# Gate products of the first 128 tokens taken ahead of the norms of the next two tiles, in an attention and gated-MLP kernel

## The chip, the cores and the metric

The kernel runs on one core of a Trainium2 chip. The metric is the device time of one execution in microseconds; the median over runs is quoted. A core has five engines, named as in the profile: PE (TensorE, matmuls; PEld is its loading of weights), DVE (VectorE), ACT (ScalarE), POOL (GpSimd) and SP (SyncE, which here issues DMA transfers). Each engine works through its own queue in order; a wait for another engine or a transfer holds everything behind it.

## The reference

Four batches of eight heads, 768 tokens, head size 64. Attention sees a window of 16 neighbours and 24 block summaries; its output goes through a norm and a gated MLP with weights 512 x 1536, 512 x 1536 and 1536 x 512.

```python
k_sum = k.reshape(B, H, nb, 32, D).max(axis=3)
v_sum = v.reshape(B, H, nb, 32, D).mean(axis=3)
scores_l = where(|i - j| < 16, q @ k.T / sqrt(D), -1e9)
scores_s = q @ k_sum.T / sqrt(D) + log(32)
a = softmax(concat(scores_l, scores_s))
x = a @ concat(v, v_sum)                          # 3072 tokens x 512
xn = x / sqrt(mean(x * x) + 1e-6) * rms_g
g = xn @ w_gate
out = (g * sigmoid(g) * (xn @ w_val)) @ w_out     # all in float32
```

## The kernel before

**Tiles and groups.** The 3072 tokens are 24 tiles of 128, six to a batch. A tile's attention gives `x` (128 tokens x 512); the norm turns it into `xT`, the transposed tile as an f16 pair of a high and a low half. The MLP works on groups of tiles, `GROUPS` = 384, 128, 256 and six times 384 tokens: group 0 is tiles 0 to 2, group 1 tile 3, group 2 tiles 4 and 5. A product of two f32 matrices is three f16 matmuls, high x high, high x low and low x high, summed in one PSUM bank.

**The first batch.** Attention of tiles 0 to 5 is done by the `su_` steps in f32. Meanwhile the gate and value weights arrive in chunks, are decoded by `decode` (ACT L542, DVE L543 and L544; ACT L570 then takes their sum of squares) and split into f16 halves by `split_gv` (L573: small matmuls L576 and L579, then ACT L589 and DVE L590). The output weights are decoded later, with the same `decode` lines and the sums of squares of `row_o` (ACT L632, DVE L629).

**The norm.** `norm_a` (L1105) takes the sum of squares of `x` (ACT L1110, DVE L1112, POOL L1113). `norm_b` (L1116) scales it (DVE L1121). For tiles 0 to 2 PE transposes it (four matmuls, L1129) into a bank `acc`, ACT casts the bank to the high half of `xT` (`copy`, recorded at L431) and DVE subtracts to get the low half (`sub`, L436).

**The gate.** `gate_val grp f T` (L1271) computes chunk f, 128 of the 1536 columns, for the T tokens of one group: 12 matmuls (L1284) for the gate and 12 for the value, each 128 columns of weights by T tokens. ACT L1291 takes the tanh, DVE L1292 and L1294 form `h`; groups 0, 1 and half of group 2 keep `h` until the output weights are ready (`halve` L1300, `project` L1306, matmuls L1316). Banks are `gv` (2) or, for odd chunks of the first two groups, `acc` (3). From group 5 on `seven` (L1206) does the products with seven block products in place of eight.

**Later batches.** Attention reads transposed f16 operands that SP fetches by transposing DMAs: `qT` (L801), `kT` (L734), `eT` (L863) and `xT` (L1137). Scores are PE L839, the product with the values PE L880. Sums over blocks of k and v are folded from tiles `hn` (`sum_load` L662, its DMA L671; `sum_fold` L674: ACT L681 and, for the v sums, POOL L687 and L692); PE L704 adds the sums of squares.

**What sets the order.** `PLAN` (L43) is a string of steps in the order in which they are recorded. `WARM` (L41) gives some steps a number of filler matmuls (L746, 128x256 of ones) that keep TensorE busy. After recording, `in_order` (L334) puts each engine's instructions into the order that `ORDER` (L148) lists for it: one table of numbers each for PE, ACT, DVE, POOL and SP. So the recorded order decides which buffers an instruction gets, and the tables decide what it is queued behind.

## Time and profile before

| | us |
|---|---|
| median of 3 runs | 706.69 |
| the runs | 705.15, 706.69, 710.21 |
| the profiled execution's own time | 705.49 |
| its span | 703.7 |

The profiled execution is 1.8 us longer than its span (what lies before the first and after the last instruction) and 1.20 us below the median. The mean granted clock of TensorE is 0.995 of full speed. PE is the busiest engine, 673.9 us or 96% of the span; DVE follows with 549.5, ACT with 494.2, POOL with 220.7. To read the profile: a row of the timeline gives start, length, engine, line, operation, output<-input, partitions x elements and, in brackets, how long the engine stood still before it and what ended that wait. Matmuls overlap: of a run of n equal ones the spacing is the run's length less one matmul's, divided by n - 1.

### The profile page before, as it was taken

Reading aid. Unit: us, or ns where it says so; the run is one execution under the profiler, and the core shown is the slowest. Engines: PE = TensorE matmul, PEld = TensorE weight load, DVE = VectorE, ACT = ScalarE, POOL = GpSimd, SP = SyncE. Lnnn points to the kernel's source line nnn. Section 1 sums busy time; section 2 is a strip of 40 time slices with the busy share of each in tenths; the row PEclk is TensorE's granted clock in tenths of the full one; section 3 lists DMA queues with packets and bytes.
Section 4 is the critical chain, followed back from the end, with each engine's and each line's share of the span. In section 5 each row is a group of like instructions: output and inputs, shape, how many; then the busy total and the mean of one; then the engine's idle time right before and its main releaser. Section 6 shows DMA issues by size and latency. Waiting matters only on the chain.

```text
span 703.7 us, 16081 instructions
## 1 busy us (share of the span) xinstructions
PE 673.9 (96%) x5854; PEld 480.9 (68%) x5854; DVE 549.5 (78%) x1611; ACT 494.2 (70%) x1083; POOL 220.7 (31%) x321
## 2 busy tenths in 40 slices
PE   7898999979989899999999999999999999999997
PEld 5585767866546665555655655877888698779874
DVE  3798889799888776757989988999887878675443
ACT  3597866668887778647677786858889767834432
POOL 4465222550334353513133533432133213410000
PEclk9999999999999999999999999999999999999999
DMA  9999562736588978767458966282949553330001
GB/s 202 287 332 283 187 211 72 130 67 113 105 162 189 164 157 162 139 143 154 104 114 161 172 149 129 64 157 59 161 80 172 130 94 62 78 51 16 32 16 46
DMA packets 243860, 93.32 MB, mean 133 GB/s; under 512 B 227717, under 2 KB 227717, under 8 KB 243781
## 3 DMA queue, kind: packets, MB, share of 16 engines
q1 hardware_dynamic: 239172, 84.78, 58.3%
q10 hardware_dynamic: 3456, 6.29, 2.5%
q0 software_dynamic: 1152, 1.22, 0.7%
q8 instruction: 46, 0.75, 0.5%
q14 instruction: 34, 0.27, 0.1%
HBM read 50.45 MB, written 6.59 MB: 81 GB/s over the span
## 4 chain that ended last, share of the span: by engine, by line
PE 65%; DVE 11%; DMA 8%; ACT 7%; issue 3%; POOL 2%; SPq 2%; ACTq 0%; DVEq 0%; POOLq 0%
PE acc L1316 18%; PE gv L1216 16%; PE gv L1284 15%; PE acc L1284 3%; DMA eT<-ee 2%; PE att L880 2%; PE att L839 2%; DMA qT<-qs 2%; PE att L1052 1%; DMA hn<-in_k_dram 1%; PE gv L746 1%; POOL ee L436 1%; DVE sm L843 1%; SPq L750 1%; DMA v2f<-in_v_dram 1%
## 5 line engine op out<-in xcount | busy, mean ns | idle before, releaser
L1316 PE MATMUL acc<-wo,hhl 128*128 128x512 f16 x864 | 228.6, 379 | 0.0
L1284 PE MATMUL gv<-xT,w_gv 128*128 128x384 f16 (+2 forms) x1296 | 215.6, 304 | 4.0 <-DVE h L1294 2.0
L1284 PEld LDWEIGHTS <-w_gv 128*128 128x128 f16 x1584 | 141.3, 99 | 77.1 <-issue 8.9
L1316 PEld LDWEIGHTS <-hhl 128*128 128x128 f16 x864 | 81.5, 98 | 61.9 <-issue 1.1
L436 POOL TENSOR_TENSOR ee<-sm,ee 128x256 f16<-128x256 f32 (+1 forms) x72 | 70.7, 995 | 164.6 <-ACT ee L431 142.5
L1216 PEld LDWEIGHTS <-w_gv 128*128 128x128 f16 x1008 | 87.3, 98 | 13.1 <-DMA xT<-xs 1.0
L854 ACT ACTIVATE sm<-sm,mx,c 128x192 f32<-128x192 f32 x144 | 70.7, 538 | 1.6
L1216 PE MATMUL gv<-S,w_gv 128*128 128x192 f16 x504 | 63.6, 246 | 0.0
L843 DVE CUSTOM_DVE_ANT_0 sm<-att,mask 128x192 f32<-128x192 f32 x144 | 44.7, 351 | 15.8 <-PE att L839 9.1
L1216 PE MATMUL gv<-xT,w_gv 128*128 128x192 f16 x504 | 55.2, 246 | 0.6 <-DMA xT<-xs 0.6
L1216 PEld LDWEIGHTS <-wo 128*128 128x128 f16 x540 | 46.9, 98 | 5.5 <-issue 0.4
L1216 PE MATMUL gv<-xT,wo 128*128 128x192 f16 x360 | 49.0, 246 | 0.0
L880 PE MATMUL att<-vv,eT 128*128 128x65 f16 x720 | 43.0, 193 | 4.8 <-DMA eT<-ee 2.4
L880 PEld LDWEIGHTS <-eT 128*128 128x128 f16 x720 | 34.6, 97 | 14.7 <-DMA eT<-ee 3.9
L839 PE MATMUL att<-kT,qT 128*128 128x192 f16 x288 | 41.2, 246 | 3.5 <-DMA qT<-qs 3.0
L1284 PE MATMUL acc<-xT,w_gv 128*128 128x384 f16 (+1 forms) x288 | 42.6, 272 | 1.9 <-DVE h L1292 1.0
L436 POOL TENSOR_TENSOR xs<-x,xs 128x512 f16<-128x512 f32 x21 | 24.5, 1167 | 49.5 <-ACT xs L431 49.4
L681 ACT ACTIVATE junk<-hn 96x512 uint8<-96x512 f32 x48 | 30.0, 624 | 10.8 <-DMA hn<-in_v_dram 6.0
L431 ACT CAST ee<-sm 128x512 f16<-128x512 f32 (+1 forms) x72 | 34.8, 507 | 1.8 <-DMA eT<-ee 1.0
L839 PEld LDWEIGHTS <-qT 128*128 128x128 f16 x288 | 25.7, 98 | 15.1 <-DMA qT<-qs 4.3
L1113 POOL TENSOR_TENSOR x_r<-x_r,consts 128x1 f32<-128x1 f32 x24 | 19.8, 826 | 49.3 <-DVE x_r L1112 41.7
L687 POOL TENSOR_TENSOR hn<-hn 96x512 f32<-96x512 f32 x18 | 24.7, 1370 | 27.5 <-DMA hn<-in_v_dram 16.5
...
## 6 DMA issues: line engine op xcount, KB each, us to landing
...
```

The costliest lines, as they stand in the source:

```text
L431: nc.scalar.copy(o, i)
L436: (nc.vector if ENG.get(op, "p") == "v" else nc.gpsimd).tensor_tensor(o, a, b, op=ALU.subtract)
L681: nc.scalar.activation(junk[0:96], y[:, o:o + DM], AF.Square, accum_out=d["ss"][:, j:j + 1])
L687: eng.tensor_tensor(x[:, 0:w], x[:, 0:w], y[:, 0:w], op=op)
L839: nc.tensor.matmul(pt[:, j * SC:(j + 1) * SC], lhsT=s["qT"][:, a * H + h, :], rhs=kT[:, h, :], start=(a == 0), stop=(a == 1))
L843: nc.vector.tensor_tensor_reduce(sm[:, i, :], pt[:, j * SC:(j + 1) * SC], mask, 1.0, NEG, op0=ALU.add, op1=ALU.max, accum_out=mx[:, i:i + 1])
L854: nc.scalar.activation(sm[:, i, :], sm[:, i, :], AF.Exp, scale=s["c"][:, 0:1], bias=mx[:, i:i + 1])
L880: nc.tensor.matmul(po[r][:, h // 2, 0:D + 1], lhsT=e, rhs=vv[:, 0:D + 1], start=(n == 0), stop=(n == len(pairs) - 1))
L1113: nc.gpsimd.tensor_tensor(r, r, nhalf, op=ALU.pow)
L1216: nc.tensor.matmul(bank[:, i * T2:(i + 1) * T2], lhsT=right(n, wi, c), rhs=left(xi, c), start=start, stop=(i == 1 and c == 1 and wi == 1), ...
L1284: nc.tensor.matmul(pt[:, 0:T], lhsT=w_gv[:, f - f % 2 + i, wi, c, f % 2, :], rhs=x[:, xi, c, 0:T], start=(n == 0), stop=(n == 3 * NC - 1))
L1316: nc.tensor.matmul(accs[grp][j], lhsT=h[:, js], rhs=wo_hl[f // 2][:, wi, f % 2, :], start=(f == first and n == 0), stop=(f == (first - 1) ...
```

## The change

- `gate_val` is taken apart into `gate_banks` (takes the PSUM banks and issues the fillers), `gate_part` (the 24 matmuls of columns a to b), `gate_head` (banks, and the part of columns 0 to 128) and `gate_val` (the rest, and all that follows).
- `PLAN` gets two steps: `gate_head 0 0` after tile 2's attention and before the norms of tiles 2 and 1, and `gate_head 0 1` after these norms. Chunks 0 and 1 of group 0 are thus computed for tile 0 first and for tiles 1 and 2 later: 48 matmuls of 128x384 become 48 of 128x128 and 48 of 128x256.
- In all gate products of `gate_part` the loop over the three half products is now outside and that over the four row blocks of the weights inside, and the low half of the tokens comes last.
- `WARM`: the fillers of `norm_b 1` and `norm_b 2` go from 8 to 4 each; the 4 of `gate_val 0 0 384` go to `gate_head 0 0`. In all 116 fillers become 108.
- The five tables of `ORDER` are new throughout. Beside these 48 matmuls and 8 fillers with their weight loads no instruction comes or goes; line numbers grow by 2, behind `gate_val` by 14.

```diff
-WARM = {... "norm_b 0": 4, "norm_b 1": 8, "norm_b 2": 8, "gate_val 0 0 384": 4}
+WARM = {... "norm_b 0": 4, "norm_b 1": 4, "norm_b 2": 4, "gate_head 0 0": 4}
-split_gv 3; su_attend 2 1; norm_a 2; norm_a 1; decode_gv 4; load_gv 10; norm_b 2; norm_b 1; su_v2 3; split_gv 4;
+split_gv 3; su_attend 2 1; gate_head 0 0; norm_a 2; norm_a 1; decode_gv 4; load_gv 10; norm_b 2; norm_b 1; gate_head 0 1; su_v2 3; split_gv 4;
 ORDER = dict(
     PE="""
-0x22 36 -37x20 4x6 -10x4 6x4 3 -4x2 8x4 -10x2 1 1 -4 7 -7 6x3 1 -2 1x3 25 -22x2 -6 5x2 4x2 15 -4 -19x3 4 17 -23 4 35
+58x2 -60x58 2 5x2 -7 1 1 -4 1 14x2 -13x2 11 -12x4 1 -2 2 -2 1 52 -49 7x2 -9x4 16 27 -28 -12 -7 -7 23 -12x2 11 1 -4 1
...
-        def gate_val(grp, f, T):
-            x = xT[grp]
+        heads = {}
+        def gate_banks(grp, f, T):
             def bank():
                 if grp < KEEP and f % 2:
                     return ps.tile([P, 512], F32, name="acc", bufs=3)
                 return ps.tile([P, 512], F32, name="gv", bufs=2)
             pg = bank()
             warm(pg)
-            pg, pv = (pg[:, 0:T], pg[:, T:2 * T]) if T <= 256 else (pg, bank())
-            for i, pt in ((0, pg), (1, pv)):
+            return (pg[:, 0:T], pg[:, T:2 * T]) if T <= 256 else (pg, bank())
+        def gate_part(grp, f, banks, a, b):
+            x = xT[grp]
+            for i, pt in enumerate(banks):
                 n = 0
-                for c in range(NC):
-                    for (wi, xi) in ((0, 0), (0, 1), (1, 0)):
-                        nc.tensor.matmul(pt[:, 0:T], lhsT=w_gv[:, f - f % 2 + i, wi, c, f % 2, :], rhs=x[:, xi, c, 0:T],
-                                         start=(n == 0), stop=(n == 3 * NC - 1))
+                for (wi, xi) in ((0, 0), (1, 0), (0, 1)):
+                    for c in range(NC):
+                        nc.tensor.matmul(pt[:, a:b], lhsT=w_gv[:, f - f % 2 + i, wi, c, f % 2, :], rhs=x[:, xi, c, a:b],
+                                         start=(n == 0), stop=(n == 3 * NC - 1), skip_group_check=True)
                         n += 1
+        def gate_head(grp, f):
+            heads[grp, f] = gate_banks(grp, f, groups[grp])
+            gate_part(grp, f, heads[grp, f], 0, P)
+        def gate_val(grp, f, T):
+            pg, pv = heads[grp, f] if (grp, f) in heads else gate_banks(grp, f, T)
+            gate_part(grp, f, (pg, pv), P if (grp, f) in heads else 0, T)
```

Place 1, PE around the transposes of tile 0 (L1129 before, L1131 after). Before, they are followed by eight fillers (L746; one pair of rows stands for them) and the small matmuls of a weight split:

```order
L1129 MATMUL acc<-ident,x 128x128 x4
L746 LDWEIGHTS ones
L746 MATMUL acc<-ones 128x256
...
L576 MATMUL att<-w_ss,ones 128x1
L579 LDWEIGHTS w_gv
L579 MATMUL att<-consts,w_gv 128x1
```

After, on PE at the same place:

```order
L1131 MATMUL acc<-ident,x 128x128 x4
L748 LDWEIGHTS ones
L748 MATMUL acc<-ones 128x256
...
L748 MATMUL gv<-ones 128x256
L1290 LDWEIGHTS w_gv
L1290 MATMUL gv<-xT,w_gv 128x128
```

Two fillers and then the first gate matmul of tile 0 stand in front of the small matmuls (now L578 and L581); the rest of the 48 follow among the later fillers, splits and transposes, and the first 128x256 one stands behind all of them.

The same place on ACT, before: three decodes (L542), the two squares of `norm_a` (L1110), then the sums of squares of the weights (L570) around the casts of `xT` (L431).

```order
L542 ACTIVATE w_985<-wo_459 128x1024
L1110 ACTIVATE junk,x_ss<-x 128x512 x2
L570 ACTIVATE w_gv,w_ss<-w_813 128x1024
L570 ACTIVATE w_gv,w_ss<-w_877 128x1024
L431 CAST xT<-acc 128x4x128
L570 ACTIVATE w_gv,w_ss<-w_985 128x1024
L431 CAST xT<-acc 128x4x128 x2
```

After, on ACT (all lines 2 higher):

```order
L544 ACTIVATE w_1025<-wo_459 128x1024
L1112 ACTIVATE junk,x_ss<-x 128x512 x2
L433 CAST xT<-acc 128x4x128
L572 ACTIVATE w_gv,w_ss<-w_843 128x1024
L572 ACTIVATE w_gv,w_ss<-w_925 128x1024
L572 ACTIVATE w_gv,w_ss<-w_1025 128x1024
L433 CAST xT<-acc 128x4x128
```

The cast of tile 0 has moved in front of two sums of squares.

Place 2, DVE where group 1's gate ends and group 2's first bank (`gv`) is waited for: the last two decodes (L544), sums of squares (L629, an ISA row each with one that reads the sum) and the products of group 1 (L1292, L1294). Before:

```order
L544 SCALAR_TENSOR_TENSOR wo_1348<-wo_1348,w_2062 128x1024
L544 SCALAR_TENSOR_TENSOR wo_1484<-wo_1484,w_2139 128x1024
L629 ISA th,scales<-wo_1072 128x512
L629 ISA scales 128x1
L1292 SCALAR_TENSOR_TENSOR h_227<-h_227,gv 128x128
L1294 SCALAR_TENSOR_TENSOR h_227<-h_227,gains,gv 128x128
```

After, on DVE (L546, L631, L1306, L1308):

```order
L546 SCALAR_TENSOR_TENSOR wo_1388<-wo_1388,w_2102 128x1024
L1306 SCALAR_TENSOR_TENSOR h_227<-h_227,gv 128x128
L546 SCALAR_TENSOR_TENSOR wo_1524<-wo_1524,w_2179 128x1024
L1306 SCALAR_TENSOR_TENSOR h_227<-h_227,gv 128x128
L631 ISA th,scales<-wo_1216 128x512
L631 ISA scales 128x1
L1308 SCALAR_TENSOR_TENSOR h_227<-h_227,gains,gv 128x128 x2
```

One sum of squares (`wo_1112`) has gone ahead of the decodes, another (`wo_1216`) has come in front of the last product L1308.

Place 3, SP around the fourth of the transposing loads of `qT`. Before:

```order
L1137 DMA_TRANSPOSE xT<-xs 128x8x128
L671 DMA hn<-in_k_dram 96x512
L734 DMA_TRANSPOSE kT<-khl 128x8x128
L863 DMA_TRANSPOSE eT<-ee 128x12x128
L671 DMA hn<-in_k_dram 96x512
L801 DMA_TRANSPOSE qT<-qs 128x16x128
```

After, on SP (L736, L1139, L673, L865, L803):

```order
L736 DMA_TRANSPOSE kT<-khl 128x8x128
L1139 DMA_TRANSPOSE xT<-xs 128x8x128
L673 DMA hn<-in_k_dram 96x512
L865 DMA_TRANSPOSE eT<-ee 128x12x128
L803 DMA_TRANSPOSE qT<-qs 128x16x128
L673 DMA hn<-in_k_dram 96x512
```

The load of `qT` is now issued in front of the second load of `hn`.

## Rows read from the trace of the kernel before

**Rows 1.** The page, part 1: busy us, share of the span, instructions of each engine.

```profile
PE 673.9 (96%) x5854; PEld 480.9 (68%) x5854; DVE 549.5 (78%) x1611; ACT 494.2 (70%) x1083; POOL 220.7 (31%) x321
```

**Rows 2.** The waits of PE, longest sums first.

```profile
PE att L576 <- ACT w_gv L570: 3.4, 3, 2.5
PE att L839 <- DMA qT<-qs: 3.0, 2, 1.7
...
PE att L704 <- ACT junk L681: 1.8, 1, 1.8
```

**Rows 3.** Windows of 2 us: PE, PEld, DVE, ACT, POOL busy, granted clock, DMA share, GB/s.

```profile
54.00:56.00 2.00, 0.00 (x0) 0.00 (x0) 2.00 (x4) 1.97 (x7) 0.15 (x1) 1.00 1.09 336
...
58.00:60.00 2.00, 2.00 (x18) 1.76 (x17) 1.81 (x7) 0.98 (x3) 0.74 (x4) 0.58 1.09 299
60.00:62.00 2.00, 2.00 (x18) 1.99 (x17) 1.12 (x4) 1.06 (x2) 1.86 (x8) 0.57 1.12 289
```

**Rows 4.** The timeline of PE, 48 to 66 us.

```profile
52.04 0.60 PE L1129 MATMUL acc<-ident,x 128*128 128x128 f32 x4
...
56.04 0.38 PE L576 MATMUL att<-w_ss,ones 128*128 128x1 f32 x2 [2.52 <-ACT w_gv L570]
...
58.80 1.06 PE L1129 MATMUL acc<-ident,x 128*128 128x128 f32 x4
...
62.27 0.33 PE L1284 MATMUL gv<-xT,w_gv 128*128 128x384 f16 x1
...
64.11 2.11 PE L1284 MATMUL gv<-xT,w_gv 128*128 128x384 f16 x12
```

**Rows 5.** The timeline of ACT, 48 to 66 us.

```profile
54.85 1.04 ACT L570 ACTIVATE w_gv<-w 128x1024 bf16<-128x1024 f32 x1
...
56.93 0.56 ACT L431 CAST xT<-acc 128x512 f16<-128x512 f32 x1
```

**Rows 6.** The timeline of PE, 141 to 158 us.

```profile
148.33 0.22 PE L1284 MATMUL gv<-xT,w_gv 128*128 128x128 f16 x1
...
148.83 1.11 PE L1284 MATMUL gv<-xT,w_gv 128*128 128x128 f16 x17
151.77 0.39 PE L704 MATMUL att<-kv_ss,ones 96*128 96x8 f32 x2 [1.82 <-ACT junk L681]
...
153.62 4.56 PE L1284 MATMUL gv<-xT,w_gv 128*128 128x256 f16 x25 [1.39 <-DVE h L1294]
```

**Rows 7.** The timeline of PE, 228 to 236 us.

```profile
228.54 1.47 PE L1284 MATMUL gv<-xT,w_gv 128*128 128x256 f16 x12
...
230.28 0.27 PE L1284 MATMUL gv<-xT,w_gv 128*128 128x256 f16 x1
232.28 0.83 PE L839 MATMUL att<-kT,qT 128*128 128x192 f16 x8 [1.73 <-DMA qT<-qs]
```

**Rows 8.** The timeline of DVE, 141 to 158 us.

```profile
146.87 4.43 DVE L544 SCALAR_TENSOR_TENSOR wo<-wo,w 128x1024 uint32<-128x1024 uint32 x2
151.22 1.75 DVE L629 CUSTOM_DVE_ANT_0 th<-wo 128x512 bf16<-128x512 f32 x1
...
153.21 0.35 DVE L1294 SCALAR_TENSOR_TENSOR h<-h,gains,gv 128x128 f32<-128x128 f32 x1
...
153.68 0.95 DVE L629 CUSTOM_DVE_ANT_0 th<-wo 128x512 bf16<-128x512 f32 x1
```

**Rows 9.** The timeline of POOL, 141 to 158 us.

```profile
146.44 1.52 POOL L687 TENSOR_TENSOR hn<-hn 96x512 f32<-96x512 f32 x1 [2.09 <-DMA hn<-in_v_dram]
147.93 1.15 POOL L436 TENSOR_TENSOR xs<-x,xs 128x512 f16<-128x512 f32 x1
```

**Rows 10.** The timeline of DVE, 48 to 66 us.

```profile
53.35 2.35 DVE L544 SCALAR_TENSOR_TENSOR w<-wo,w 128x1024 uint32<-128x1024 uint32 x2
```

**Rows 11.** The timeline of SP's DMA queue, 206 to 226 us.

```profile
224.17 0.76 SPq L671 DMA_DIRECT2D hn<-in_k_dram  x1
225.01 3.96 SPq L801 DMA_TRANSPOSE qT<-qs  x1
```

More of the change, by code (lines that the diff above doesn't have):

```diff
@@ new lines @@
+-11x3 8x4 -12x2 10 -107 -55 2 44 6 105 -111 -3 2 3 -4 117x5 7 -8 7x3 -10 9 -10x5 5 -24 -116 138x4 2 3 -4 -29 28x2 1x3
+-41 6 -7 29x2 -29 54 -52 -7 44 12 3 -4x3 -16 50 89 -121x2 -6 5 -6 -26 58 10x2 -12x3 9x2 -11 10x2 -112 111 -51 37x3 10
+-11x3 -39x2 5x2 -13 -25 29x2 5 -6x2 4x2 -6 10 -6x5 1 3 24 -75 45x3 1x4 -57 147 -148 5 70 -75 74 69 -142 5x2 -5x3 -5
+142x3 -5 -71x3 68 -69x2 70 -71x2 6 -7 20 -21 5 -6x2 4x2 -6 -82 5 75 4x8 4 -5x2 4x2 10x3 -19 27 -10 9 -10 9x2 -29 111x2
+2 -88 -12x4 8x2 -10x3 -18 106x2 1x3 -88x5 -34 4 -5 5 -6x2 2 1 108 -57 11x2 -13x3 10x2 -12x4 8 -9x3 6 -36 2 -3 27 6x4
@@ new lines @@
+191 -54 53 -13x3 10 -11 -188 197 -11 10x2 -12 11 -12 11 -12 11x2 -66 3 -4x2 3 11x2 33 -47 -3 3 -2 45 -40 39 10 -51 -5x2
+-4 11 -12 5 -4 52 -45 -4 5 2 -3 4 -3 2 -6 2 48 -46 -12x2 -5 12 46x4 -49 1 46 -18 17x3 -20 19 -20 19x2 -21x9 24x12
+-24x12 24x12 -24x12 24x10 -22 21 -22 21 -22x10 24x6 -143 142x2 -20x3 17 -18x2 16 -17x3 14 -15x4 11 -147x3 -4 147x4 -155
+162 -9x4 5 -6 5 -6 5 -6x2 4x2 6 -7x6 4 -4 3 -4x2 2x2 58x2 10 -11x2 9 -10 9 -10x3 7x2 -9 8x3 -11 10 -11 -69 68 -69x5 4
+-5 72x3 -42x2 40x4 -44 43 7 -8x2 -78 77 5 -6x4 2 -90x2 34 -32x2 -5 4x3 3x4 -7x3 4x3 3x2 -5x3 5 -4 3x3 -6x2 4 57 -49
@@ new lines @@
+3x3 -6x2 -121x2 119 5 -3x2 1 41x2 10x4 -14 13 -14 -172 14 111x3 42 -157 156 11 -12x2 10 -11x3 8x2 -54x4 -9x4 5 -6 -122
+131x2 -7 6 -7 6 -7 6 -7 35 9 -46 -152 196x2 -198 14x2 6 -7 2 177x2 10 -11x5 6 -7x2 5 -6x3 3 44x2 2x4 -6x2 -48 7 -8x3
+5x4 -9x2 7 -8x2 6x6 -72 -7 2x2 73 11 -12 11x2 -13x3 10x2 -12x3 9x2 -92 -5 95 -12 11 -12x3 9x3 -100 4x2 110 11x2 -13x2
+-113 123 -12x2 10x2 -12x2 10x2 -12x2 75 -76x3 7x3 -126 125 -130 130x2 -3 2x3 -132 131x7 -142 -4 6 -4 -4 143 11 -12x4 8
+-9x4 5 -6x3 37x4 5x2 -7 6 -7 6x2 5x2 -15 14x2 -16 15 5x3 -24 23 -19x2 17 -18x3 5x5 5x5 -73x3 -57 62 -7x4 3 -4 3 -4
@@ new lines @@
+-8 5 2 -16 2 5 6 -13 -24x2 22 8 4 4 -3 -5 -117 104 12 2 -3 4 -2 -9 12 -3x2 1 8 -14 5 10 1 -15 8 -8 -25 36 -12 5 -32 36
+-6 19 -4 -16 6 8 -6 -20 13 1x2 7 -6 7 -2 -7 -21 16 -6 -2 17 9 -12 -8 15 -7 2 -3x2 2 6 -4 -6 2 -38 39x2 2 1 -4 4 -2 -3 4
+-2 5 -27 27 -6x2 2 -6 6 3 -4 4 -11 11 1 -4 1 -5 -4 9 -2 5 1 -7 -11 10 3 -81 76 5x2 -7 3 2 1x2 12 -16 3 8 -11 1 8 -3 4
+-2 2 -2 4 -4x2 3 -2 -19 15 8 -5 -2 -19 -2 20 4 -5x2 4 -4 6 -30 23 6 -5 -2 1 8 -39 32x2 -4 3 4 -5 -35 34 1 6 1 -7 -2 1 5
+-6 2 -3 4 1 -2 1 4 -5 4 -5x3
@@ new lines @@
+-79 85 -8 33x3 -115 91x2 -14 34 -37 20 -3x2 1 -8 7 -8 22 -3 -14 -23x2 36x2 -4 -14 1 -2 1x2 -13 24 -25 11x2 31 -7 164
+-178 5 2 -3 2 167 -168 -4 -22 13 21 155 -163 -5 -11 10 -11 -3 12x2 163 -157x3 7 -30 29 -9 -6 13 11 -82 51x2 28 -12 -40
+28 10x2 140 -161 7 20 -20 5 5 -12 8 2 -3 -13 33 144 -148 18 -31 -7x2 13x2 -10 5x2 -13 162 -148 147 -179 34 -14x2 18x2
+1x2 -3 2 3x2 -21 20 -21 35 -15 1 -8 5 -33 -4 157 -30 -97 5 -3 2 -3 -40 15x2 142 -110 -2 -22 -16 37x3 -36 35 14 -29 -25
+1 35 2x2 -4 3 -4 -16x2 -24 69 -23 5 60 -57 -5 -13 16 10 -10 -2 -12 -10 47 -48 -18x2 29 12 -46 63 -45 27 -9 -2 1 42
@@ L330 @@
+-23 1 1 29 1 3x2 -19 28 1x2 -29 9 10 -7 -4 26 -11 -19 10 14 -36 40 -2 -2 -24x2 -15 14 2 -7 13 1x2 -3 3 8 -11 10 -21 13
+-3 24 -20 -15 24 10 -13 10 -15 -2 -4x2 3 -4 26 -9 -16 10 13x2 2 -26 1 2 17 -14 9 -6 10 -24x2 -6 1 25 -14 1 7 4 -12 -7 4
+-5 16 -3 3 -2 1
 """,
```

318 lines of the change are left out of this document (146 added, 172 removed).

## The prediction

> **What bounds the kernel now.** I first read the busy shares [rows 1]: PE is busy for 673.9 of 703.7 us, so 29.8 us of standing still, and what PE's own work can shrink, are all there is to win. Next the waits of PE [rows 2]. The largest one, 3.4 us in three waits, is for ACT's sums of squares of the weights (L570); then come 3.0 us for the transposed queries and 1.8 us for the sums of squares of `hn`. Everything else is many waits of a microsecond or less. Then the windows around the first of these [rows 3]: from 54 to 56 us PE does nothing, while DVE (2.00), ACT (1.97) and the DMA engines (1.09) are full; right behind the wait PE is busy again, but at a granted clock of 0.58 and 0.57, the lower of its two levels (1.2 and 2.4 GHz). The reader is to see that this stage is bound by ACT and DVE, which decode weights, and that PE sits there with work that is not ready. The timelines [rows 4, 5] say why: tile 0 is transposed at 52.04, but its cast starts only at 56.93 behind sums of squares; the transposes of the other tiles come from 58.80, and the solid run of gate products starts at 64.11. Later, around 150 us, PE waits again, 1.82 us for ACT and 1.39 us for DVE [rows 6].
>
> **The change part by part.**
>
> *Gate products moved ahead.* 24 matmuls for each of chunks 0 and 1 are cut at column 128. Spacing, as run less one matmul over n - 1: 128x384, (2.11 - 0.33) / 11 = 0.162 us [rows 4]; 128x256, (1.47 - 0.27) / 11 = 0.109 us [rows 7]; 128x128, (1.11 - 0.22) / 16 = 0.056 us [rows 6]. So 48 x (0.056 + 0.109 - 0.162) = +0.14 us of work is added, but 48 x 0.056 = 2.7 us of it goes to a place where PE waits, and 48 x (0.162 - 0.109) = 2.5 us leaves the run behind 62 us. When can the heads run? By the new order on ACT the cast takes the place of the first L570, which started at 54.85 [rows 5]; with its 0.56 us the high half is there at 55.4; the low half comes from DVE after that, and the loop now asks for it last. That leaves 6.6 us up to 62 for heads that need 2.7. The sums of squares come 0.56 us later, and with them the splits of the next weights; the products that need those weights come behind, so I cost it at nothing, and 0.56 us if that cover is gone. Value -2.5 us; bounds -2.5 and 0 (a later wait takes it all).
>
> By the Trainium skill ("TensorE: Matmul & The Clock Gate", section "Back-to-back issue gap") pairs of a weight load and a matmul of 128 columns sustain about 81 ns each, which speaks against cutting matmuls small. Such pairs run here at 56 ns, so the trace does not agree; by the page the heads would take 48 x 0.081 = 3.9 us, an estimate; where the wait doesn't hide the 1.2 us more, the sum below would be -1.2 in place of -2.4.
>
> *Fillers.* Eight fewer of 0.109 us (the 128x256 spacing) are 0.9 us, but some lie beside waits. Bounds -0.9 and 0; I take -0.4.
>
> *Clock.* The half-clock stretch covers about the two windows 58 to 62 us [rows 3], so at most half of its time is lost, about 1.7 us. The wait in front of the first head, from 52.8 (transposes and two fillers) to 55.4, is as long as the 2.52 us before, so I expect the fall to the lower clock to stay, only earlier. Bounds -1.7 (it goes) and +1.7 (a second such stretch); value 0.
>
> *DVE at 142 to 154 us.* PE waits for L1294, which frees the bank of group 2's first product [rows 6, 8]. In the new order one sum of squares (L629) has moved ahead of the two decodes and another one stands before the last L1294, so between the same points DVE does one more L629, 0.95 to 1.75 us, and one more product of 128x128, for which I take L1294's 0.35 [rows 8]. Queued behind it on DVE are further sums of squares only; waiting for it is PE. Upper bound +2.1; I take 0.95 + 0.35 = +1.3, by the L629 that is nearest to what the engine does alone. The lower bound comes from POOL. The two decodes took 4.43 us at 146.87, while POOL ran L687 and L436 [rows 8, 9]; two of the same kind took 2.35 us at 53.35, with POOL busy for only 0.15 us of the window 54 to 56 [rows 3, 10]. If the new order parts them, 2.1 us go: lower bound -2.1.
>
> The Trainium skill ("SBUF — State Buffer", section "SBUF: two separate sides") says that DVE and POOL share a port pair which one instruction holds to its end while the other blocks. The trace agrees: 4.43 against 2.35 us. By it a pair of decodes that meets no POOL work gets the whole 2.1 us back, and the sum below would be -4.5.
>
> *Transposed queries.* PE waited 1.73 us for the load at 225.01 [rows 7, 11]. In the new SP order it is issued ahead of an `hn` load of 0.76 us, so it can land about 0.8 us sooner: -0.8. Bounds -3.0 (both waits of [rows 2] go) and 0.
>
> *Everything else that is reordered.* The rest of the tables shifts instructions by one or two microseconds of their own engine's work. Existing waits may shrink and new ones of the same size (a few tenths to one microsecond) may come in the middle of the program. I see no sign that holds for the sum: 0, with +-3 us as the size of a few such waits.
>
> **Sum.** -2.5 - 0.4 + 0 + 1.3 - 0.8 = -2.4 us. Against the profiled execution's own 705.49 us that is 703.1. That execution lies 1.20 us below the median of 706.69, so the median to expect is 703.1 + 1.2 = 704.3 us. The best bounds add to -10.2, the worst, with the products' gain lost, to +3.8, each without the +-3 of the rest.
>
> **The rivals.**
>
> *Absorbed.* The stage at 142 to 154 us may not follow PE at all: ACT's L681, for which PE waited 1.82 us, waits for `hn`, whose chain of loads and POOL folds runs by itself [rows 2, 6, 9]. Then the 2.9 us won at 62 are waited off there, while the other terms stay at +1.3 - 0.8. Time 705.5 + 0.5 + 1.2 = 707.2. For it: POOL waits 2.09 us for `hn` in the middle of that chain. Against it: DVE there has hardly any idle time, and it starts on products that PE delivers.
>
> *Faster.* The decodes lose their collision with POOL (-2.1) and both query waits go (-3.0), beside -2.9 from the head and no L629 term: 705.5 - 8.0 + 1.2 = 698.7. For it: every start on the way is a few microseconds earlier, so the collision, which is an accident of time, is as likely to go as to stay. Against it: all three must happen.
>
> *Slower.* One mechanism: DVE at 142 to 154 us. If `hn` fixes the start, the extra L629 runs beside POOL at 1.75 us with its 0.35 us product, and PE waits 1.39 + 2.1 us at one place; behind a wait of that length the clock fell before, so a longer stretch at half clock costs up to another 1.7 us. Time 705.5 + 3.8 + 1.2 = 710.5. It decides as soon as L1294 ends later than 153.6 us. Against it: the other sum of squares went ahead, to where DVE may have room.
>
> *The change doesn't do what it says.* The low clock may meet the heads: 48 at half clock cost 2.7 us more, splits and transposes with them, and the run behind 62 us starts late by what it saves. The others leave -0.4 + 1.3 - 0.8 = +0.1. Time 705.5 + 0.1 + 1.2 = 706.8. For it: the wait ahead of the heads stays. Against it: 6.6 us of room.
>
> **How the numbers follow.** My forecast has a chance of 0.42, absorbed 0.23, faster 0.15, slower 0.12, low clock at the heads 0.08. About 1%, 7.1 us, is what a measurement of this kernel tells from no change: faster is below 699.6, slower above 713.8. Faster takes two thirds of the faster case and a fifth of the forecast's, whose spread of 3 us reaches there: 0.18. Slower takes a third of the slower case and a little of the others with the rest's +3 us: 0.06. The rest, 0.76, is within 1%. The range, 698.0 to 709.5, reaches to the middle of the faster and almost to the slower case; the likeliest case's own is 701.3 to 707.3, its time with the 3 us either way.
>
> **What would show it.** Right: the first gate product near 55.5 us behind a wait of 2 to 3 us, the cast before L570 on ACT, the solid run behind 62 us shorter by 2.5 us, PE ahead by 2 to 3 us at 66 us and still by 1 to 2 at 154; the L629 in front of L1294 as the last thing PE waits for there; a wait for `qT` near 230 us of about 0.9 us. Wrong: no lead at 66 us (heads late, or at half clock); a lead that is gone at 152 us (absorbed); decodes of 2.4 us a pair at 147 us (faster); new waits above 1 us in the middle of the program, which I could not see.

## The result, and the profile after

| set | before, us (runs) | after, us (runs) | ratio after / before, 95% interval |
|---|---|---|---|
| first | 707.98 (20) | 700.82 (20) | 0.9909 (0.9887 to 0.9931) |
| second | 704.8 (17) | 702.15 (11) | 0.9940 (0.9912 to 0.9968) |

The change makes the kernel a little faster: by 0.91% (0.0091 x 707.98 = 6.4 us) in one set of runs and 0.60% (4.2 us) in the other, both inside the 1% that the prediction called no change. The ratio compares all runs and is not the quotient of the two medians, which is 0.9899 in the first set and 0.9962 in the second, both inside the intervals; a gain in us below is the ratio's unless it is said to be between medians. The profiled execution of the first set was the slowest of its 20 (707.55 us), so the rows below are those of the second set's, called e1, whose own time of 702.18 us is close to its median. Its span is 700.4 us, against 703.7 before.

Where did the 3.3 us between the two profiled executions come from? I cut the trace at two marks that both kernels have: PE's first matmul of `project` (L1316, L1330 after) and its first of `seven` (L1216, L1218 after). In e1 they stand here (the rows of PE on one line, with the first and last start behind the durations):

```profile
L1330 PE MATMUL acc<-wo,hhl x20: 376/379/379, 166.0 to 171.9; 128*128 128x512 f16 x20
L1218 PE MATMUL gv<-xT,w_gv x9: 243/246/246, 442.3 to 443.0; 128*128 128x192 f16 x9
```

| us | to the first L1316 | from there to the first L1216 | from there to PE's last matmul |
|---|---|---|---|
| before | 164.40 | 277.86 | 257.26 |
| e1 (after) | 166.03 | 276.30 | 253.89 |
| difference | +1.63 | -1.56 | -3.37 |

So the stage that holds the heads and everything that I had worked out but the queries took 1.6 us *longer*, and the gain lies in the two stages for which I had written no more than the -0.8 us of the queries. For the last one the waits of PE say why. Before, from 442 us to the end:

```profile
PE att L880 <- DMA eT<-ee: 1.5, 3, 0.7
PE gv L1216 <- DMA xT<-xs: 0.6, 1, 0.6
PE att L839 <- DVE hhl L1268: 0.5, 1, 0.5
```

In e1, over the same stretch, there is one row:

```profile
PE gv L1218 <- DVE th L1306: 0.5, 1, 0.5
```

Of the 2.6 us of small waits for transposing loads and for DVE nothing is left inside the stage: e1's one wait ends with the first L1218 itself, just ahead of the mark. PE's busy time in the stage fell as well, from 254.67 to 253.69 us, in part because a few products of other lines (two of L1284 and six of L880 in the trace) now run ahead of the mark; the rest of the 3.37 us isn't traced to a row.

**The views that answer to those of before.** Busy time of e1 [rows 1], with 40 more matmuls (48 heads less 8 fillers):

```profile
PE 675.3 (96%) x5894; PEld 485.9 (69%) x5894; DVE 553.9 (79%) x1611; ACT 493.0 (70%) x1083; POOL 226.3 (32%) x321
```

The waits of PE in e1, longest first [rows 2]. The 3.4 us for the sums of squares of the weights have shrunk to 0.2; a wait of 2.0 us for the cast of `xT` has come in their place, and waits for DVE's products are now the largest:

```profile
PE gv L1290 <- DVE h L1308: 2.4, 2, 1.9
PE gv L1290 <- DVE th L1306: 2.2, 2, 1.9
PE gv L1290 <- ACT xT L433: 2.0, 1, 2.0
PE att L706 <- ACT junk L683: 1.9, 3, 1.1
PE att L841 <- DMA qT<-qs: 1.7, 1, 1.7
```

The timeline of ACT at the heads [rows 5]: the cast of tile 0 now starts 2.96 us earlier than before and ahead of the first L572, as the order said.

```profile
53.97 0.56 ACT L433 CAST xT<-acc 128x512 f16<-128x512 f32 x1
54.44 1.06 ACT L572 ACTIVATE w_gv<-w 128x1024 bf16<-128x1024 f32 x1
```

The timeline of PE there [rows 4]: the first head at 54.59 behind a wait of 2.04 us, the first 128x256 product at 63.98 (one of the 48 head matmuls, at 64.63, comes behind it).

```profile
51.16 0.60 PE L1131 MATMUL acc<-ident,x 128*128 128x128 f32 x4
...
54.59 0.22 PE L1290 MATMUL gv<-xT,w_gv 128*128 128x128 f16 x1 [2.04 <-ACT xT L433]
...
59.55 1.06 PE L1131 MATMUL acc<-ident,x 128*128 128x128 f32 x4
...
63.98 0.27 PE L1290 MATMUL gv<-xT,w_gv 128*128 128x256 f16 x1
```

There is no lead behind them. The first tanh of a gate product on ACT, which waits for PE in both kernels, starts in e1 and before at

```profile
67.45 0.58 ACT L1305 ACTIVATE h<-gv,gains 128x384 f32<-128x384 f32 x1 [0.21 <-PE gv L1290]
```

```profile
66.59 0.58 ACT L1291 ACTIVATE h<-gv,gains 128x384 f32<-128x384 f32 x1 [0.26 <-PE gv L1284]
```

And the windows [rows 3]: behind that wait PE has work in every window, but at a granted clock of 0.50, its lower level (1.2 GHz), up to 62 us; before, that stretch covered 58 to 62. Four matmuls of L1131 take 1.06 us in it and 0.60 outside.

```profile
54.00:56.00 2.00, 1.24 (x15) 1.03 (x15) 2.00 (x5) 1.58 (x4) 1.57 (x2) 0.96 0.54 131
56.00:58.00 2.00, 2.00 (x17) 1.47 (x17) 2.00 (x4) 1.18 (x3) 0.55 (x1) 0.50 1.22 249
58.00:60.00 2.00, 2.00 (x25) 1.91 (x23) 1.77 (x8) 1.12 (x2) 0.33 (x3) 0.50 0.99 318
60.00:62.00 2.00, 2.00 (x15) 1.94 (x14) 0.69 (x1) 1.35 (x2) 1.79 (x7) 0.50 1.05 334
```

What the clock takes in the whole first stage shows in longer windows, whose length times what the granted clock lacks to 1 is the full-speed time that is lost. In e1:

```profile
0.00:52.00 52.00, 47.25 (x345) 35.26 (x346) 36.20 (x136) 32.91 (x54) 28.82 (x72) 0.97 1.04 277
52.00:66.00 14.00, 11.51 (x114) 10.18 (x114) 11.10 (x23) 9.89 (x18) 6.23 (x15) 0.76 0.94 281
...
132.00:160.00 28.00, 22.78 (x265) 21.27 (x263) 23.19 (x56) 16.48 (x41) 16.40 (x19) 0.88 0.40 89
```

52 x 0.03 + 14 x 0.24 + 28 x 0.12 = 8.3 us, in three stretches (about 10 to 15, 56 to 63 and 144 to 152 us). Before, in the same windows:

```profile
0.00:52.00 52.00, 46.13 (x341) 34.69 (x342) 36.05 (x136) 32.77 (x54) 26.12 (x70) 1.00 1.03 272
52.00:66.00 14.00, 10.85 (x93) 8.56 (x92) 11.52 (x31) 10.06 (x18) 4.98 (x14) 0.88 1.03 271
...
132.00:160.00 28.00, 23.27 (x281) 20.92 (x279) 24.43 (x72) 19.79 (x49) 13.78 (x18) 0.94 0.58 105
```

0 + 14 x 0.12 + 28 x 0.06 = 3.4 us. The 5 us between them lie on the path only where PE has work, but they are more than the heads were to bring. The stretch at the heads comes in every profile of the new order with heads and no more fillers: from 52 to 66 us the granted clock is 0.77 in the first set's profiled execution and 0.76 in e1 and in e7, e10 and e11 below. The one at 10 to 15 us doesn't: in e7, e10 and e11 it is 1.00 up to 52 us.

The second place, PE from 139 to 160 us [rows 6]:

```profile
143.38 0.33 PE L1290 MATMUL gv<-xT,w_gv 128*128 128x128 f16 x3 [1.88 <-DVE h L1308]
145.57 2.18 PE L1290 MATMUL acc<-xT,w_gv 128*128 128x128 f16 x19 [1.08 <-DVE h L1308]
155.12 0.39 PE L706 MATMUL att<-kv_ss,ones 96*128 96x8 f32 x2 [1.09 <-ACT junk L683]
155.99 4.20 PE L1290 MATMUL gv<-xT,w_gv 128*128 128x256 f16 x37 [0.49 <-DVE h L1308]
```

Before, two waits for L1294 stood at the places of the first two:

```profile
142.38 0.27 PE L1284 MATMUL gv<-xT,w_gv 128*128 128x128 f16 x2 [0.64 <-DVE h L1294]
144.59 0.66 PE L1284 MATMUL acc<-xT,w_gv 128*128 128x128 f16 x9 [0.88 <-DVE h L1294]
```

With the 1.82 and 1.39 us of [rows 6] that makes 4.73 us before and 4.54 in e1: the wait at the last L1308, where I had put +1.3 us, fell from 1.39 to 0.49, and the first one rose from 0.64 to 1.88. (Just ahead, at 136.84, e1 has a wait of 0.67 us for ACT that before hasn't.) DVE there [rows 8] still loses one decode to POOL, 3.29 us against 1.26 for the next one, of the same shape:

```profile
148.03 3.29 DVE L546 SCALAR_TENSOR_TENSOR wo<-wo,w 128x1024 uint32<-128x1024 uint32 x1
...
153.07 0.29 DVE L1306 SCALAR_TENSOR_TENSOR h<-h,gv 128x128 f32<-128x128 f32 x1 [1.74 <-ACT h L1305]
153.27 1.26 DVE L546 SCALAR_TENSOR_TENSOR wo<-wo,w 128x1024 uint32<-128x1024 uint32 x1
```

beside the same pair of POOL operations [rows 9]:

```profile
147.70 1.43 POOL L689 TENSOR_TENSOR hn<-hn 96x512 f32<-96x512 f32 x1 [2.17 <-DMA hn<-in_v_dram]
149.09 1.14 POOL L438 TENSOR_TENSOR xs<-x,xs 128x512 f16<-128x512 f32 x1
```

### The profile page after: what moved, and what is told of

Same layout as the page of the kernel before. It is cut to its first block, busy times and chain, and to the rows that moved or that the text cites. A ratio compares the mean times of both kernels' runs of the same rounds, so it can differ in the third digit from the quotient of the medians.

```text
span 705.8 us, 16168 instructions
## 1 busy us (share of the span) xinstructions
PE 675.3 (96%) x5894; PEld 484.6 (69%) x5894; DVE 550.6 (78%) x1611; ACT 493.4 (70%) x1083; POOL 224.9 (32%) x321
## 4 chain that ended last, share of the span: by engine, by line
PE 53%; DMA 13%; DVE 13%; ACT 11%; POOL 4%; issue 4%; SPq 2%; ACTq 0%; POOLq 0%; DVEq 0%
PE gv L1218 19%; PE acc L1330 15%; PE gv L1290 9%; DMA hn<-in_v_dram 4%; DMA hn<-in_k_dram 3%; ACT sm L856 2%; PE att L841 2%; PE att L882 2%; SPq L752 2%; DMA eT<-ee 1%; DMA v1f<-in_v_dram 1%; POOL hn L689 1%; ACT junk L683 1%; ACT hhl L1317 1%; POOL ee L438 1%
## 5 line engine op out<-in xcount | busy, mean ns | idle before, releaser
L1330 PE MATMUL acc<-wo,hhl 128*128 128x512 f16 x864 | 234.6, 379 | 0.9 <-ACT hhl L1317 0.7
L1290 PE MATMUL gv<-xT,w_gv 128*128 128x384 f16 (+2 forms) x1320 | 219.0, 302 | 6.8 <-DVE th L1306 2.2
L1290 PEld LDWEIGHTS <-w_gv 128*128 128x128 f16 x1632 | 146.0, 99 | 76.6 <-issue 9.4
L1330 PEld LDWEIGHTS <-hhl 128*128 128x128 f16 x864 | 81.6, 98 | 59.3 <-DVE hhl L438 1.1
L1218 PEld LDWEIGHTS <-w_gv 128*128 128x128 f16 x1008 | 87.1, 98 | 10.3 <-issue 0.3
L1218 PE MATMUL gv<-S,w_gv 128*128 128x192 f16 x504 | 64.7, 246 | 0.0
L1218 PE MATMUL gv<-xT,w_gv 128*128 128x192 f16 x504 | 54.0, 246 | 0.0
L1218 PEld LDWEIGHTS <-wo 128*128 128x128 f16 x540 | 47.0, 98 | 6.9 <-issue 0.9
L1218 PE MATMUL gv<-xT,wo 128*128 128x192 f16 x360 | 49.4, 246 | 0.1
L1290 PE MATMUL acc<-xT,w_gv 128*128 128x128 f16 (+2 forms) x312 | 44.0, 266 | 1.9 <-DVE h L1308 1.1
L438 POOL TENSOR_TENSOR xs<-x,xs 128x512 f16<-128x512 f32 x21 | 26.2, 1249 | 52.4 <-ACT xs L433 46.1
L1115 POOL TENSOR_TENSOR x_r<-x_r,consts 128x1 f32<-128x1 f32 x24 | 16.9, 707 | 59.1 <-DVE x_r L1114 52.6
L433 ACT CAST ee<-sm 128x256 f16<-128x256 f32 (+1 forms) x72 | 34.8, 508 | 1.4 <-DMA eT<-ee 0.7
```

The costliest lines, as they stand in the source:

```text
L433: nc.scalar.copy(o, i)
L438: (nc.vector if ENG.get(op, "p") == "v" else nc.gpsimd).tensor_tensor(o, a, b, op=ALU.subtract)
L1115: nc.gpsimd.tensor_tensor(r, r, nhalf, op=ALU.pow)
L1218: nc.tensor.matmul(bank[:, i * T2:(i + 1) * T2], lhsT=right(n, wi, c), rhs=left(xi, c), start=start, stop=(i == 1 and c == 1 and wi == 1), ...
L1290: nc.tensor.matmul(pt[:, a:b], lhsT=w_gv[:, f - f % 2 + i, wi, c, f % 2, :], rhs=x[:, xi, c, a:b], start=(n == 0), stop=(n == 3 * NC - 1), ...
L1330: nc.tensor.matmul(accs[grp][j], lhsT=h[:, js], rhs=wo_hl[f // 2][:, wi, f % 2, :], start=(f == first and n == 0), stop=(f == (first - 1) ...
```

## The experiments

My theory after the result: the gain comes from the new tables, late in the program, and the lead of the heads is lost on the way. The rivals: the heads carry the gain; or the new loop order in the gate products does. Ratios are to the kernel before, run on the same chip in the same batch; the four batches ran on four chips. Times are medians, with the number of runs. A line has other numbers in other kernels: in e8, e10, e11 and e12 they are 2 higher than in e1.

**First batch: the parts one at a time.** Before: 704.8 us. e1 is the changed kernel again.

> The changed kernel once more, for a second profile: the first one is of a 707.55 us execution, far above the median of 700.82, with a mean granted clock of 0.987 where others of it show 0.993. Theory A (the prediction's: the heads win 2.5 to 3 us at 62 us, the rest of the new order about nothing): an execution near 700 shows a lead of 3 us at 66 us and the remainder of the 6 to 7 us as shorter waits at many places. Theory B (the five new tables win most, the heads little): the lead at 66 us is under 2 us and grows at named waits between 140 and 560 us. Theory C (the clock): the span less what half clock costs is the same as that of the kernel before, and the gain is fewer half-clock stretches. By C a 700 us execution has a higher mean clock than the 0.995 of before; by A and B it may have a lower one. Median expected 700 to 702.

Measured: 702.15 us (11), 0.9940 (0.9912 to 0.9968). Faster, by less than in the first set.

*e2, heads alone.* The heads, the fillers and the earlier cast of tile 0 in the tables of before; the new loop order comes with `gate_part`.

```diff
 PLAN of before
+gate_head 0 0; ... gate_head 0 1
 ORDER of before
+the 48 heads where the changed kernel has them; the cast of tile 0 ahead of the first L570
+for (wi, xi) in ((0, 0), (1, 0), (0, 1)):
```

> The 48 head matmuls with the new loop order, the 8 fillers fewer and the earlier cast of tile 0, but elsewhere the order of the kernel before on all five engines. Theory A: most of the gain is here, -2.5 to -4 us (703.5 to 705.5 at a before of 708). Theory B: 0 to -2 us, since a lead at 62 us is waited off at 152 us, where the stage hangs on hn loads and DVE. Theory C: as B, with a mean clock that explains the difference.

Measured: 718.3 us (6), 1.0175 (1.0134 to 1.0215): far slower.

*e3, tables alone.* The new tables, fillers and loop order, no heads.

```diff
 the changed kernel
-gate_head 0 0; ... gate_head 0 1
```

> The five new order tables and the 8 fillers fewer with the new loop order, but no heads: chunks 0 and 1 of group 0 are computed whole, 128x384, where the changed kernel has its 128x256 parts. Theory A: 0 to -3 us against before (705 to 708), 3 us slower than the changed kernel. Theory B: -4 to -6 us (702 to 704), within 2 us of the changed kernel. In this order the wait for the first gate product at 52 to 62 us has fewer instructions to fill it, so a longer wait there (4 to 6 us) is expected by both.

Measured: 700.15 us (7), 0.9909 (0.9870 to 0.9947): as much as the changed kernel's gain in either set, without the heads.

*e4, loop order alone.*

```diff
 the kernel before
-for c in range(NC):
-    for (wi, xi) in ((0, 0), (0, 1), (1, 0)):
+for (wi, xi) in ((0, 0), (1, 0), (0, 1)):
+    for c in range(NC):
```

> The kernel before with the new loop order alone (products of the tokens' high half first in every gate_val); all else as before. Both theories: within 1 us of before, since by the profile no gate product waited for the low half of xT; A would have it at 0, B at 0 to -1 us. A gain of 2 us or more would mean that the loop order itself carries part of the gain.

Measured: 715.06 us (4), 1.0127 (1.0071 to 1.0183). A pure exchange among the 12 matmuls of each product costs 9 us, and so explains most of e2's 12 us. One place of the loss is the timeline of ACT in e4, where L1182 writes the block sums of `seven` over gate weights that PE must have read:

```profile
332.20 0.41 ACT L1182 CAST w_gv<-S 128x256 f16<-128x256 f32 x1 [3.56 <-PE gv L1284]
...
334.10 0.41 ACT L1182 CAST w_gv<-S 128x256 f16<-128x256 f32 x1 [1.20 <-PE gv L1284]
```

Before, the same two casts waited less:

```profile
331.50 0.41 ACT L1182 CAST w_gv<-S 128x256 f16<-128x256 f32 x1 [1.25 <-PE gv L1284]
332.40 0.41 ACT L1182 CAST w_gv<-S 128x256 f16<-128x256 f32 x1 [0.20 <-PE gv L1284]
```

PE issues the same matmuls in both at this place, in e4 even 1.29 us earlier, so against PE's work the first cast is 2.0 us late. What it overwrites are row blocks 0 and 1 of a chunk's weights, in the high half first (`first = w[:, :, 0:2, 1]` in `make_t`). In the old loop the 5th of a product's 12 matmuls is the last to read these, in the new one, which comes back to the high half for the tokens' low half, it is the 10th. The tanh of the next product stands behind the casts on ACT, and PE pays in e4's timeline (the other places of the loss were not read):

```profile
339.35 0.48 PE L1284 MATMUL gv<-xT,w_gv 128*128 128x384 f16 x2 [3.39 <-DVE th L1292]
```

**Second batch: which part of the tables, and the loop undone.** Before: 707.81 us.

*e5.* e2 with the old loop order but for the two head chunks.

```diff
 e2
-for (wi, xi) in ((0, 0), (1, 0), (0, 1)): ...
+the old order, where (grp, f) not in heads
```

> The kernel before with the heads of chunks 0 and 1, the earlier cast of tile 0 and 8 fillers fewer, the new loop order only within these two chunks and the old loop order everywhere else: the run with the new loop order everywhere was 13.5 us slower than before, of which 10 are the loop order's. Theory A (heads worth 2.5 to 3 us): 701.5 to 703 at a before of 704.8. Theory B (the lead is waited off later, as the pair of changed kernel and tables without heads suggests, where a lead of 6.5 us at 80 us was down to 1.7 us at 440 us): 704 to 706, the same as before within 1 us, with a lead of 2 us or more at 100 us that is gone by 160 us.

Measured: 706.37 us (12), 0.9980 (0.9954 to 1.0006). Heads, cast and fewer fillers without the new tables: 0.0020 x 707.81 = 1.4 us, which can't be told from nothing.

*e6, the late order alone.* Before's order up to the first gate product of group 2, the new tables behind it.

```diff
 ORDER of before, up to the first product of gate_val 2
+ORDER of the changed kernel behind it; new loop order for grp >= 2
```

> The kernel before up to the first gate product of group 2 (no heads, old loop order, old order of the steps before it, at about 153 us), and behind it the new order of all five engines with the new loop order from group 2 on. Theory B (the tables win behind 153 us): -4 to -7 us, 698 to 701 at a before of 704.8. Theory A: 0 to -2 us. The lead over the kernel before should be 0 at 150 us and grow between 160 and 440 us.

Measured: 713.46 us (6), 1.0102 (1.0065 to 1.0139). I had hoped to see the gain alone. The middle stage, where the two orders meet, costs more (286.50 us against 277.86 before, in the table below) than the late order wins; the waits of PE from 164 to 451 us begin with

```profile
PE att L841 <- DMA qT<-qs: 5.0, 3, 4.0
```

But behind 450.6 us, where its `seven` begins, e6 has hardly a wait left:

```profile
PE att L841 <- DMA qT<-qs: 0.2, 1, 0.2
```

and that stage takes 254.13 us, as in the changed kernel, with an early part that is before's.

*e7, the changed kernel with the old loop order* (but in the head chunks).

```diff
 the changed kernel
-for (wi, xi) in ((0, 0), (1, 0), (0, 1)): ...
+the old order, where (grp, f) not in heads
```

> The changed kernel with the old loop order everywhere except in the two chunks with heads; its five tables are kept. If the tables suit the new loop order only, 4 us or more slower than the changed kernel (706 or more), with a new wait of ACT L1184 or DVE L1185, which write S over the weights, for the last gate product. If the old loop order is the better one under any table (it reads each high half of the weights for the last time earlier), 0 to 2 us faster than the changed kernel (700 to 702).

Measured: 700.57 us (12), 0.9922 (0.9893 to 0.9951): as the changed kernel. The loop order costs 9 us under the old tables and nothing that can be told from the runs under the new ones, so it is no gain of its own: the old tables bear only the old loop order, the new ones bear both.

e7 and e5 differ in nothing but the five tables, and they ran in the same batch. Between their medians lie 5.8 us (700.57 and 706.37), and nine of e7's twelve times lie below the fastest of e5's twelve (703.78). This is the most direct measure of the tables in the series, with the heads in both kernels.

The stages of all kernels, in their profiled executions (the marks by the lines of before):

| us | to the first L1316 | to the first L1216 | to the last matmul |
|---|---|---|---|
| before | 164.40 | 277.86 | 257.26 |
| e2 heads alone | 165.36 | 294.12 | 256.20 |
| e4 loop alone | 162.78 | 289.92 | 258.17 |
| e5 heads, old loop | 168.88 | 279.46 | 255.56 |
| e6 late order | 164.10 | 286.50 | 254.13 |
| e1 after | 166.03 | 276.30 | 253.89 |
| after, the first set's | 170.18 | 277.37 | 254.07 |
| e3 tables alone | 169.56 | 274.44 | 253.89 |
| e7 after, old loop | 164.11 | 274.73 | 254.11 |
| e8 after, 16 fillers | 161.36 | 280.14 | 254.19 |
| e9 tables, 18 fillers | 163.19 | 277.17 | 254.92 |
| e10 two places undone | 165.67 | 276.53 | 253.90 |
| e11 products early | 164.90 | 275.34 | 254.12 |
| e12 e8 and e11 | 163.07 | 279.02 | 253.90 |

The last column parts the kernels cleanly: 255.6 to 258.2 with the old late order, 253.9 to 254.9 with the new one. The first two don't add up: who is early in the first is mostly late in the second. They are single executions, too: the two of the changed kernel differ by 4.15 us in the first column, 1.07 in the second and 0.18 in the third, and those of e3 and e8 are the slowest of their runs. So the first column alone tells little. e3's 169.56, for one, holds a stretch at half clock from 34 to 46 us, ahead of tile 0's transposes, which start at 55.99 there and at 51.16 in e1.

**Third batch: the clock, and the two other terms.** Before: 705.15 us.

*e8.* 16 more fillers in the wait ahead of the first head, so that PE doesn't stand still there.

```diff
 the changed kernel
-"gate_head 0 0": 4
+"gate_head 0 0": 20
```

> The changed kernel with 16 more fillers (1.7 us at full clock) between tile 0's transposes and the first head, where PE stood still for 2.04 us in its profiled execution and ran at half clock for 6 to 8 us from about 55 us on. If that wait is what makes the clock fall there, the stretch at half clock goes and 3 to 4 us are won: 697 to 699 at a changed kernel of 700.8 to 702. If the clock falls for another reason (or the fillers only count as more of the same), 0 to +1 us: 701 to 703.

Measured: 699.82 us (6), 0.9901 (0.9865 to 0.9937), between the two cases that I had set apart. The stretch at half clock behind the wait is gone (e8's windows, as above):

```profile
52.00:66.00 14.00, 12.92 (x156) 11.27 (x155) 12.59 (x30) 11.57 (x21) 8.11 (x17) 1.00 0.93 275
...
132.00:160.00 28.00, 21.54 (x246) 19.21 (x243) 24.49 (x72) 20.51 (x50) 12.83 (x14) 0.94 0.44 95
```

PE reaches L1316 at 161.36, 4.67 us earlier than in e1 and 3.04 earlier than before: about the lead that I had forecast for the heads, with the clock kept. Not all of it is the heads': tile 0's transposes, ahead of any head, start at 50.40 in e8, 51.16 in e1 and 52.04 before, so 1.6 us of the lead over before comes from ahead of them. In this execution, the slowest of the six, the lead over e1 was gone by 340 us. First at 326, where the timeline of PE has

```profile
326.10 0.65 PE L1292 MATMUL gv<-xT,w_gv 128*128 128x384 f16 x3 [2.03 <-DVE th L1308]
```

a wait that traces back to ACT, which could not overwrite `ee` before a transposing load had read it:

```profile
324.06 0.92 ACT L435 CAST ee<-sm 128x256 f16<-128x256 f32 x2 [2.82 <-DMA eT<-ee]
```

In e1 the same cast starts at 325.22, only 1.16 us later, without a wait: of e8's lead of 3.9 us at this place the rest had been spent on waiting for the load. And behind the wait the clock falls in e8, where e1 stays at 1.00:

```profile
328.00:330.00 2.00, 2.00 (x8) 0.91 (x6) 2.00 (x9) 0.39 (x1) 0.00 (x0) 0.50 1.00 189
```

*e9.* The fillers without the heads.

```diff
 e3
-"gate_val 0 0 384": 4
+"gate_val 0 0 384": 22
```

> The new tables without heads, with 18 more fillers in the wait of 2.77 us before the first sum over weight squares. In the run without them that wait was followed by some 10 us at half clock (5 us lost). If the wait makes the clock fall: 696 to 698 against 700.15 without the fillers, which would leave the heads worth less than nothing. If not: 700 to 702.

Measured: 702.68 us (12), 0.9956 (0.9926 to 0.9986), above both cases. The clock is kept here too (1.00 from 52 to 66 us, as in e8), so e8 against e9 tells what the heads are worth where the clock doesn't fall: 2.9 us between the medians. The intervals of the two ratios overlap, but the kernels ran on one chip in one batch, and five of e8's six times lie below the fastest of e9's twelve (700.74 us). The profiles say how: from tile 0's transposes to the first gate product behind the heads (in e9, the first gate product of all) PE waits 1.49 us in e8 and 3.28 in e9, and it reaches L1316 at 161.36 and 163.19. Without these fillers no gain shows: e1 against e3, in the first batch, has the heads at a loss of 2.0 us between the medians, with times that overlap widely (696.89 to 703.91 and 697.38 to 703.83).

*e10, two places undone.* The extra L631 behind the last L1308 on DVE; the fourth load of `qT` behind the next of `hn` on SP.

```diff
 DVE
-L631 th<-wo_1216
 L1308 h<-h,gains,gv x2
+L631 th<-wo_1216
 SP
-L803 DMA_TRANSPOSE qT<-qs
 L673 DMA hn<-in_k_dram
+L803 DMA_TRANSPOSE qT<-qs
```

> The changed kernel with two places put back: on DVE the sum of squares row_o 2 goes behind the last product L1308 (the prediction gave it +1.3 us), on SP the fourth load of qT goes behind the next load of hn (the prediction gave the new order -0.8 us). By the prediction's sizes: PE's wait near 156 us for L1308 (0.49 us in the changed kernel) goes, and a wait for qT of about 0.8 us appears near 230 us; the total is 0 to -1 us. By what the trace of the changed kernel shows the two are small change: within 1 us in total, no wait for qT near 230 us longer than 0.4 us.

Measured: 701.82 us (10), 0.9950 (0.9921 to 0.9978), the same as e1. On SP the undone place brings back a wait of the size that I had given it:

```profile
231.51 0.92 PE L843 MATMUL att<-kT,qT 128*128 128x192 f16 x9 [0.79 <-DMA qT<-qs]
```

In e1 PE has no wait there. Neither has it the other wait of [rows 2] for `qT`; but a later load is late, in e1 and in e10 alike, where before had no wait:

```profile
273.66 0.26 PE L841 MATMUL att<-kT,qT 128*128 128x192 f16 x1 [1.72 <-DMA qT<-qs]
```

On DVE nothing is won: PE waits 0.69 us in place of 0.49, and the profile puts this wait down to the sum of squares itself (L633 here), which now stands behind the last product:

```profile
154.44 7.08 PE L1292 MATMUL gv<-xT,w_gv 128*128 128x256 f16 x48 [0.69 <-DVE scales L633]
```

The last product had ended at 153.56 (two of L1310 from 152.96, 0.60 us), so to put the sum behind it didn't free PE of the sum; why, the profile doesn't show. What the sum costs in e1 is thus bounded by the wait of 0.49 us there, not by e10's time.

*e11.* Two products of DVE, for which PE waits 1.88 us at 143 in e1, right behind the subtotals they use.

```diff
 DVE
 L1306 h<-h,gv x2
+L1308 h<-h,gains,gv x2
 L1099, L1100, L1101 ...
-L1308 h<-h,gains,gv x2
```

> The changed kernel with two DVE products L1308 (chunks 4 and 6 of group 1) moved ahead of the copy of kT and the attention outputs L1101, right behind their L1306. PE waited 1.88 us for them near 143 us. If DVE's order there is what swallows the heads' lead, the wait goes and 1 to 2 us are won (699.5 to 701 at 701.5). If the lead is lost to the whole stage up to 156 us (the next waits for ACT L683 and for L1308 follow at 145 to 156 us), the wait moves there and the total stays within 0.5 us.

Measured: 700.14 us (6), 0.9912 (0.9879 to 0.9945). The wait is gone, and the two next to it have grown in its place (the timeline of PE in e11):

```profile
145.03 1.22 PE L1292 MATMUL acc<-xT,w_gv 128*128 128x128 f16 x19 [3.12 <-DVE h L1310]
153.44 0.39 PE L708 MATMUL att<-kv_ss,ones 96*128 96x8 f32 x2 [2.72 <-ACT junk L685]
```

3.12 + 2.72 = 5.84 us here, against 4.54 in e1 for the whole place: what DVE gives is waited off for DVE's next product and then for the sums of squares of `hn`. In the same batch e11's median lies 1.7 us below e10's, though, so the products may be worth something in all.

**Fourth batch.** Before: 705.31 us.

*e12: e8 and e11 together,* to see whether the two leads add.

```diff
 e8
+the DVE order of e11
```

> The changed kernel with both edits: 16 more fillers in the wait before the first head, and the two products L1308 moved ahead of the attention outputs. If each frees what the other one loses again between 139 and 156 us, 697 to 698.5, the best of the series. If that stage is set by the chain of hn loads (PE's wait for ACT L683), which no edit here touches, 699 to 701, as with either edit alone, with a wait of 2.5 us or more for L683 near 150 us.

Measured: 700.73 us (12), 0.9925 (0.9892 to 0.9957). They don't add, as far as these intervals tell. The wait for the sums of `hn`, which I had put at 2.5 us or more, is 1.09 us (at 150.48), so that this chain sets the stage isn't shown. The best median is e8's, but its interval holds the ratios of the changed kernel's first set, e3, e7 and e11, and its second set's (0.9940) lies just outside; no version is shown to beat the changed one.

## Why the prediction was right or wrong

**The time.** 704.3 us was forecast, 2.4 below the 706.69 of then; measured were 700.82 (ratio 0.9909) and 702.15 (0.9940). Range and class hold; by the ratios the gain is 2 to 4 us larger than the sum, and most of it doesn't come from where the sum put it. That the time fell into the range is luck as much as working: the largest gain of the sum isn't there in e1, its one loss (+1.3) didn't come either, and most of what came had been written as 0.

**Gate products moved ahead, -2.5: the step that failed, by its room and by the clock.** Each local part came: the cast early, the heads at 54.59, a wait of 2.04 us. But there was no lead at 66 us, which I had named as a sign of being wrong: the first tanh behind a gate product starts at 67.45 (L1305), against 66.59 before (L1291). Two things were wrong. The 6.6 us of room up to 62 were not free: from 58 us on PE had been busy before as well (2.00 in each window of [rows 3]). What stood still there were 2.52 and 0.63 us, most of the 3.4 us of [rows 2], and 2.04 us came back as the wait for the cast. And the heads ran at half clock and filled the time to 63.98, not to 62, so the first stage came out 1.63 us longer than before's. This is the rival of the low clock, to which I gave 0.08, and which forecast 706.8 for want of any other gain. With the clock kept the heads win about what I had put: 2.9 us in the medians (e8 against e9). Where it falls no run shows a gain of theirs: the tables win as much without heads (e3), and heads without tables win 1.4 us at best guess (e5).

The rival "absorbed", to which I gave 0.23, is not what happened in e1, which had no lead to absorb. Of e8 it tells half: PE's waits from 139 to 156 us are 4.73 us before, 4.54 in e1, 5.96 in e8 and 5.84 in e11, so work that is ready earlier there meets longer waits, but e8's lead passed the place and was lost in the middle stage of that one execution (280.14 us against 277.86 before).

**Fillers, -0.4: not shown apart.** No run changes these eight alone. Fillers did more as clock keepers (e8) than as time to be saved.

**Clock, 0 with bounds of 1.7 either way: mechanism right, size wrong.** The fall stayed and came earlier, as put. But in the window 52 to 66 us it loses 14 x 0.24 = 3.4 us of full-speed time, against 1.7 before: the 1.7 more are the upper bound, not the middle, and the heads ran in it. The second stretch, at 144 to 152 us, doubled as well in e1 (28 x 0.12 against 28 x 0.06), for which I had no term; in the first set's profiled execution it is smaller than before's (28 x 0.03).

**DVE at 142 to 154 us, +1.3: not paid.** The last wait there fell from 1.39 to 0.49 us, so the sum of squares in front of it costs 0.49 at most; e10 can't tell, as its wait ends with the same sum. DVE had stood still for 1.74 us up to 153.07, waiting for ACT, in the midst of the work that I had summed. I had added durations in front of one wait without asking whether DVE was idle between them.

**Transposed queries, -0.8: right where it was put** (0.79 us come back in e10). Of the 3.0 us of [rows 2] the new tables as a whole leave 1.7, at another place (273.66), which the exchange on SP doesn't cause, as e10 has it too.

**Everything else, 0: the mis-sized term.** The middle stage measured -1.56 us and the last one -3.37, -4.9 in all; without the 0.8 of the queries that is -4.1. The bound of 3 us was set for the whole of it, by a few waits, and this lies outside. By e5 against e7 the tables are worth 5.8 us with heads in both kernels; e3, without heads, says much the same. The waits of before from 442 us on, 2.6 us in all, would have shown what there was to win. I had looked at the three places that the order made easy to read. I had also missed that the loop order had a price of its own: 9 us in e4 under the old tables, which the new ones hide.

**What stays open.** Which engine's table carries the late gain: kernels with one engine's table undone were not tried. What the heads are worth in the changed kernel itself, where the clock falls: e1 and e3 don't tell. And why a lead at 164 us isn't kept to 442: e8 shows one way (a transposing load, then the clock) in one execution, not that it is the only one. Why the second set's gain came out smaller than the first's, 4.2 against 6.4 us, wasn't looked into; the two intervals overlap.
